# Retention in chunks, then eight experts: states multiplied in four quarters, the last logits in one go, and row writes moved earlier

## The chip, the cores and the metric

One core of a Trainium2 chip runs one program. The metric is device time in microseconds (us): the median over runs of the time of the whole program. One more execution was recorded by the profiler; every row and every time of a stage below is from that execution, counted from its first instruction.

## What is computed

The first half is a linear attention with decay (retention); the second is a layer of experts in which the pairs of token and expert are served in the order of their logits, each expert takes exactly 384 tokens, and each token goes to one expert.

```python
gamma = 1.0 - 2.0 ** (-5.0 - np.arange(H))            # B, H, S, D = 4, 8, 768, 64
for t in range(S):
    state = gamma * state + einsum('bhd,bhe->bhde', k[:, :, t], v[:, :, t])
    y[:, :, t] = scale * einsum('bhd,bhde->bhe', q[:, :, t], state)
x = y.transpose(0, 2, 1, 3).reshape(N, H * D)         # N = 3072 tokens of 512
logits = x @ w_gate                                   # E = 8 experts, cap = N // E = 384
for idx in np.argsort(-logits.flatten()):             # token idx // E, expert idx % E:
    ...                                               # taken if the token is free and counts[e] < cap
for e in range(E):
    out[assigned == e] = np.maximum(x[assigned == e] @ w1[e], 0) @ w2[e]
```

## The kernel before

**Units.** A sequence of 768 tokens is cut into six chunks of 128. A unit is one chunk of one of the four batches; unit u is chunk u // 4 of batch u % 4, so units 0 to 3 are the first chunk and 20 to 23 the last. `load(u)` brings a unit's keys, queries, values and keys again (1 MB; 768 KB in the last chunk) into one of eight buffers `ld`. Load u + 8 is issued when unit u is done, from SP, the one queue that also issues everything else of this stage.

**A unit's work.** `scores` multiplies keys with queries (TensorE, `sc`, two halves of the rows side by side), VectorE multiplies that with the decay (`am`), GpSimd scales queries and keys for the state (`qs`, `ks`). `outputs` multiplies the state `T[b]` with `qs` into the PSUM tile `yp`: per pair of heads a 128x128 matrix with the two heads' 64x64 states on its diagonal and zeros elsewhere. `mix` adds the values times `am` into the same tile, ScalarE copies it to `YS`, and keys times values go into `sp`, from which VectorE adds the next state into `T[b]`, in two instructions of 64 partitions per unit. The heads lie on partitions and the tokens on columns, so `YS` is the transposed x.

**Order.** TensorE, VectorE and ScalarE run in the written order of the loop over `groups`: eight groups of one unit, then eight of two. In each turn the scores of the next group are issued first, then `outputs`, then `aside()` (a small step of the routing), then `mix`. `gate(c)` makes the logits of a whole chunk with four matmuls side by side in 32 columns each; `gate_last` makes those of the last chunk unit by unit, 8 columns wide.

**Rows.** x has to lie in DRAM as rows, since the experts gather tokens from there. `row_blocks` turns 14 of the 24 units on VectorE into `xr` (a ring `xo` of six) and issues four writes of 64 KB each, called pieces below; `ROWS` says after which group. The other ten units are turned on TensorE (`row_out`) beside the first search for a threshold (`BESIDE`).

**Routing.** `span_parts` finds the range of the logits from the first `KNOWN` chunks; a search in three steps of 64 thresholds finds an expert's threshold, its tokens are numbered, x and the weights are gathered. After the last chunk comes the first count (`c0`), then the rest of the first search, which `BESIDE`, `HOT` and `WARM` fill with work or with multiplications of constants. From then on TensorE works through the eight experts, with the later searches beside it.

The SP queue gives each DMA one of eight semaphores in turn, so the ninth DMA in order waits until the first has landed.

Of the kernel before, what the change touches and what calls it, by code (L numbers as in the profile page):

```python
# [22 lines left out]
E = 8  # L23
# [23 lines left out]
LEFT = sum(k for k, _ in BESIDE)  # L47
# [6 lines left out]
def tile_retention_moe(ctx: ExitStack, tc: tile.TileContext, qkv, wg, idm, w1, w2,  # L54
# [15 lines left out]
    wgf = consts.tile([128, HP, 32], F32, name="wgf")  # L70
# [20 lines left out]

    def consts_on_chip():
        nc.vector.memset(onesb, 1.0)
# [5 lines left out]
        nc.vector.memset(un, 1.0)  # L99
        nc.vector.memset(zer512, 0.0)  # L100
        nc.vector.memset(Sc, 0.0)
        nc.vector.memset(Wq, 0.0)
        nc.vector.memset(bad, 0.0)
# [137 lines left out]
    xo = yctx.enter_context(tc.tile_pool(name="xo", bufs=6, side="right"))  # L241
# [9 lines left out]
    T = [rc.tile([128, HP, 128], F32, name=f"T{b}") for b in range(B)]  # L251
# [38 lines left out]
    def scores(u):  # L290
# [10 lines left out]
        qs = ks = None  # L301
        if c < NC - 1:
# [3 lines left out]
        if c:  # L306
            qs = rw.tile([128, HP, C], F32, name="qs", bufs=4)
            nc.gpsimd.tensor_tensor(qs.rearrange("p a b -> p (a b)"), q_,
                                    qtb[:, c].rearrange("p a b -> p (a b)"), op=OP.mult)
# [7 lines left out]

    def outputs(us):

        c = units[us[0]][1]  # L320
        for u in us:
            yp = yps[u] = rp.tile([128, HP, C], F32, name="yp", bufs=2)
            if c:
# [4 lines left out]
            else:  # L328
                busy(WARM[u + 1], yp[:, 0:2, :].rearrange("p a b -> p (a b)"))

    def mix(us):

        c = units[us[0]][1]
        for u in us:
            b, am, yp = units[u][0], st[u][0], yps.pop(u)
            v_ = LD[u][:, 2].rearrange("p (h d) -> p h d", h=H)
            for pr in range(HP):
                for s in range(2):
                    nc.tensor.matmul(yp[64 * s:64 * s + 64, pr, :], v_[:, 2 * pr + s, :], am[:, s, pr, :],  # L339
# [7 lines left out]
        if c < NC - 1:  # L347
# [13 lines left out]
    lt5 = []  # L361

    def gate_last(b):
        if not b:
            lt5.append(rp.tile([128, 64, E], F32, name="sp"))
        for pr in range(HP):
            nc.tensor.matmul(lt5[0][:, b, :], YS[b, NC - 1][:, pr, :], wgf[:, pr, 0:E], start=(pr == 0),
                             stop=(pr == HP - 1))
# [10 lines left out]
    def row_out(pr_, i):  # L379
        b, c = units[i]  # L380
        xr = xo.tile([128, DM], F32, name="xr")
        nc.scalar.activation(blocks(xr), pr_.rearrange("p (b a r) -> p b a r", a=4, b=HP), AF.Copy)
# [3 lines left out]
    def row_blocks(i):  # L386
# [6 lines left out]
        for a in range(4):  # L393
            nc.sync.dma_start(xs[t0:t0 + 128, 128 * a:128 * a + 128].rearrange("(t c) f -> c t f", t=4),
                              xr[32 * a:32 * a + 32].rearrange("p (t f) -> p t f", t=4))

    def gate(c):

        gl = rp.tile([128, 512], F32, name="gl")
        for pr in range(HP):  # L400
            for b in range(B):
                nc.tensor.matmul(gl[32 * b:32 * b + 32, 0:C], wgf[:, pr, :], YS[b, c][:, pr, :], start=(pr == 0),  # L402
# [23 lines left out]
    rowed = 0  # L426
    nu = len(units)
    groups = [[u] for u in range(2 * B)] + [[u, u + 1] for u in range(2 * B, nu, 2)]

    def aside():  # L430

        nonlocal parts, whole, ended
        if ended is not None:
            c, ended = ended, None
            logit(c)
            if c == 0:
                consts_on_chip()
# [726 lines left out]
```

## Time and profile before

| | |
|---|---|
| median of 3 runs | 443.43 us (442.95 to 445.39) |
| the profiled execution | 445.22 us, of which the span of its instructions 443.4 us |
| TensorE busy | 427.8 us (96%), granted clock 0.995 on average |
| VectorE, ScalarE, GpSimd busy | 300.8, 142.2, 142.9 us |
| retention, up to the first count's result | 0 to 104.8 us |
| first search, gathers | 104.8 to 124.2 us |
| eight experts | 124.2 us to the end |

The time around the span is 1.8 us in the profiled execution. TensorE is busy in nearly all of the span, so the chain of waits runs over it almost everywhere; but the stages have other limits beside it, which the rows below show. A row of the timeline gives the start, the length, engine, line, operation, the tiles written and read, the shapes, how many instructions are merged, and in brackets how long the engine had been idle and what ended that.

### The profile page before, as it was taken

Reading aid. Unit: us, or ns where it says so; the run is one execution under the profiler, and the core shown is the slowest. Engines: PE = TensorE matmul, PEld = TensorE weight load, DVE = VectorE, ACT = ScalarE, POOL = GpSimd, SP = SyncE. Lnnn points to the kernel's source line nnn. Section 1 sums busy time; section 2 is a strip of 40 time slices with the busy share of each in tenths; the row PEclk is TensorE's granted clock in tenths of the full one; section 3 lists DMA queues with packets and bytes.
Section 4 is the critical chain, followed back from the end, with each engine's and each line's share of the span. In section 5 each row is a group of like instructions: output and inputs, shape, how many; then the busy total and the mean of one; then the engine's idle time right before and its main releaser. Section 6 shows DMA issues by size and latency. Waiting matters only on the chain.

```text
span 443.4 us, 9124 instructions
## 1 busy us (share of the span) xinstructions
PE 427.8 (96%) x3745; PEld 372.2 (84%) x3747; DVE 300.8 (68%) x714; ACT 142.2 (32%) x221; POOL 142.9 (32%) x154
## 2 busy tenths in 40 slices
PE   9998999899989999999899999999999999999994
PEld 7887999898579778977797798789779989989983
DVE  1668689976798759875885888588668926416500
ACT  1111121203245226313431432434244436326301
POOL 2475665110340170034116216134103615402001
PEclk9999999998999999999999999999999999999999
DMA  7999888744673265138126436425703732831001
GB/s 256 410 414 417 328 261 259 215 92 132 237 231 127 97 191 236 27 133 312 54 95 218 186 120 212 169 59 167 296 26 119 229 152 77 302 143 47 1 25 53
DMA packets 23332, 78.99 MB, mean 178 GB/s; under 512 B 3058, under 2 KB 10866, under 8 KB 16884
## 3 DMA queue, kind: packets, MB, share of 16 engines
q0 software_dynamic: 8592, 46.14, 29.8%
q1 hardware_dynamic: 14692, 32.20, 20.7%
q8 instruction: 31, 0.51, 0.5%
q14 instruction: 17, 0.14, 0.1%
HBM read 65.75 MB, written 12.58 MB: 177 GB/s over the span
## 4 chain that ended last, share of the span: by engine, by line
PE 72%; issue 12%; DVE 9%; POOL 2%; DMA 1%; ACT 1%; POOLq 0%; SPq 0%; DVEq 0%
PE ph L869 22%; PE py L890 21%; PE psm L128 6%; PE sc L297 5%; PE yp L339 4%; PE yp L326 3%; PE ph L837 3%; PE sp L353 2%; DVE am L300 2%; POOL out L898 1%; PE gl L314 1%; DVE w2l L128 1%; POOL wraw L785 1%; DMA xg<-xs,idx 1%; PE gl L402 1%
## 5 line engine op out<-in xcount | busy, mean ns | idle before, releaser
L869 PE MATMUL ph<-xh,w1h 128*128 128x384 f32 x256 | 84.3, 343 | 0.5 <-ACT xh L842 0.5
L869 PE MATMUL ph<-xlo,w1h 128*128 128x384 f32 x256 | 82.7, 337 | 1.7 <-DVE xlo L128 1.5
L869 PE MATMUL ph<-xh,w1l 128*128 128x384 f32 x256 | 82.1, 335 | 0.0
L890 PE MATMUL py<-w2h,hh 128*128 128x512 f32 x192 | 78.9, 411 | 0.0
L890 PE MATMUL py<-w2l,hh 128*128 128x512 f32 x192 | 75.4, 393 | 0.6 <-DVE w2l L128 0.6
L890 PE MATMUL py<-w2h,hl 128*128 128x512 f32 x192 | 75.3, 392 | 0.0
L898 POOL DMA_INDIRECT out<-yo,oix x24 | 28.4, 1182 | 125.4 <-ACT yo L896 124.8
L873 ACT ACTIVATE hh<-ph 128x384 fp32r<-128x384 f32 x64 | 31.4, 491 | 77.5 <-PE ph L869 75.8
L785 POOL DMA_INDIRECT wraw<-w,wix x31 | 34.4, 1109 | 51.1 <-DVE un L128 38.1
L869 PEld LDWEIGHTS ph<-xlo,w1h 128*128 128x128 f32 x256 | 47.5, 188 | 2.3 <-DVE xlo L128 2.3
L869 PEld LDWEIGHTS ph<-xh,w1h 128*128 128x128 f32 x256 | 47.8, 188 | 1.6 <-ACT xh L842 0.7
L869 PEld LDWEIGHTS ph<-xh,w1l 128*128 128x128 f32 x256 | 47.7, 188 | 0.0
L128 DVE SCALAR_TENSOR_TENSOR hl<-ph,hh 128x384 fp32r<-128x384 f32 x64 | 34.7, 552 | 16.9 <-ACT hh L873 16.6
L128 DVE TENSOR_TENSOR w1l<-wraw,w1h 128x1024 fp32r<-128x1024 f32 (+1 forms) x36 | 39.2, 1099 | 7.1 <-ACT w1h L803 7.1
L890 PEld LDWEIGHTS py<-w2h,hl 128*128 128x128 f32 x192 | 36.0, 188 | 7.8
L890 PEld LDWEIGHTS py<-w2l,hh 128*128 128x128 f32 x192 | 36.2, 188 | 7.6 <-DVE w2l L128 1.7
L896 ACT ACTIVATE yo<-py 128x512 f32<-128x512 f32 x24 | 14.4, 598 | 86.6 <-PE py L890 47.1
L890 PEld LDWEIGHTS py<-w2h,hh 128*128 128x128 f32 x192 | 36.1, 188 | 6.9 <-issue 0.7
L824 POOL DMA_INDIRECT xg<-xs,idx x24 | 27.6, 1149 | 43.3 <-PE ph L869 28.7
L128 DVE TENSOR_TENSOR w2l<-wraw,w2h 128x1024 fp32r<-128x1024 f32 x32 | 38.7, 1217 | 1.7 <-ACT w2h L803 1.7
L803 ACT ACTIVATE w1h<-wraw 128x1024 fp32r<-128x1024 f32 (+1 forms) x36 | 33.7, 959 | 7.8 <-DMA wraw<-w,wix 7.8
L300 DVE TENSOR_TENSOR am<-sc,dm 128x512 f32<-128x512 f32 x48 | 30.1, 684 | 5.1 <-PE sc L297 4.7
(145 smaller groups left out, 613.2 us busy)
## 6 DMA issues: line engine op xcount, KB each, us to landing
ld<-qkv SPq DMA_DIRECT2D x19, 1024.0 KB, 9.5
xs<-xr SPq DMA_DIRECT2D x56, 64.0 KB, 3.9
ld<-qkv SPq DMA_DIRECT2D x4, 768.0 KB, 5.8
xs<-xr SPq DMA_DIRECT2D x10, 256.0 KB, 2.8
qtb<-qtab SPq DMA_DIRECT2D x5, 256.0 KB, 11.5
ld<-qkv SPq DMA_DIRECT2D x2, 512.0 KB, 5.2
wraw<-w,wix POOLq DMA_INDIRECT x33
xg<-xs,idx POOLq DMA_INDIRECT x24
```

Source lines behind the costliest of these rows:

```text
L128: return f(o, *a, **k)
L297: nc.tensor.matmul(sc[s][:, pr, :], k_[r, w], q_[r, w], start=True, stop=True)
L300: nc.vector.tensor_tensor(am[:, s], sc[s], dm[:, s], op=OP.mult)
L339: nc.tensor.matmul(yp[64 * s:64 * s + 64, pr, :], v_[:, 2 * pr + s, :], am[:, s, pr, :], start=(not c and pr == 0), stop=(pr == HP - 1), s ...
L785: nc.gpsimd.indirect_dma_start(out=t, out_offset=None, in_=w1v if nm == "w1" else w2v, in_offset=bass.IndirectOffsetOnAxis(ap=wix[:, hf:hf ...
L803: nc.scalar.activation(p[0], p[2], AF.Copy)
L824: nc.gpsimd.indirect_dma_start(out=t, out_offset=None, in_=xs, in_offset=bass.IndirectOffsetOnAxis(ap=found[n][0][:, j:j + 1], axis=0))
L869: nc.tensor.matmul(ph, a[:, o:o + 128], x_[:, d], start=(k == 0), stop=(k == 11))
L873: nc.scalar.activation(hh[:, f], ph, AF.Relu)
L890: nc.tensor.matmul(py, h_[:, f, t], a[:, o:o + DM], start=(k == 0), stop=(k == 23))
L896: nc.scalar.activation(yo, py, AF.Copy)
L898: sct = nc.gpsimd.indirect_dma_start(out=out, out_offset=bass.IndirectOffsetOnAxis(ap=oix[:, j:j + 1], axis=0), in_=yo, in_offset=None, bo ...
```

## The change

- `T[b]` holds the two heads' states one above the other in 64 columns. `outputs` multiplies each 64x64 state by itself: rows 0 to 63 or 64 to 127 of the array, and output partitions that are swapped for odd batches (`half`), so that the two units of a group address four different quarters. VectorE's addition is one instruction of 128 partitions. For odd batches the heads in `YS` are swapped; `wgf` has a second copy with swapped rows, and the row writes swap back.
- `gate_last` is gone; the last chunk has `gate(5)`, a copy by ScalarE and one transpose, with parts of the first count between them.
- Groups of two begin with the second chunk (14 groups instead of 16). `xo` has ten buffers. `ROWS` is {6: 4, 7: 1, 8: 3, 9: 2, 11: 2, 12: 2} instead of {8: 2, 9: 2, 10: 3, 11: 1, 12: 3, 14: 3}; the order of units is `TURNED`. One of the ten later units is turned right after the last logits, so `BESIDE` has nine.
- The range comes from two chunks. Zeros and ones are set at the very start, the casts of constants after the first chunk's last group. `qs` is issued before `ks`. `WARM` falls from (10, 4, 4, 4, 0) to (10, 2, 0, 0, 0), `HOT` rises from 22 to 25.

```diff
-WARM = (10, 4, 4, 4, 0)
+WARM = (10, 2, 0, 0, 0)
-KNOWN = 3
+KNOWN = 2
-ROWS = {8: 2, 9: 2, 10: 3, 11: 1, 12: 3, 14: 3}
-HOT = 22
-BESIDE = ((4, 0), (1, 0), (4, 0), (1, 0), (0, 6), (0, 10))
+ROWS = {6: 4, 7: 1, 8: 3, 9: 2, 11: 2, 12: 2}
+HOT = 25
+BESIDE = ((4, 0), (1, 0), (4, 0), (0, 1), (0, 6), (0, 10))
+TURNED = (1, 3, 5, 0, 7, 2, 4, 9, 11, 6, 13, 15, 17, 19)
...
-    T = [rc.tile([128, HP, 128], F32, name=f"T{b}") for b in range(B)]
+    T = [rc.tile([128, HP, D], F32, name=f"T{b}") for b in range(B)]
...
+    def half(s, b):
+        o = 64 * (s ^ (b & 1))
+        return slice(o, o + 64)
...
-                for pr in range(HP):
-                    nc.tensor.matmul(yp[:, pr, :], T[b][:, pr, :], qs[:, pr, :], start=(pr == 0), stop=False,
-                                     skip_group_check=True)
+        for pr in range(HP if c else 0):
+            for u in us:
                 b, qs = units[u][0], st[u][1]
+                for s in range(2):
+                    r = slice(64 * s, 64 * s + 64)
+                    nc.tensor.matmul(yps[u][half(s, b), pr, :], T[b][r, pr, :], qs[r, pr, :], start=(pr == 0),
+                                     stop=False, skip_group_check=True)
...
-                for s in range(2):
-                    r = slice(64 * s, 64 * s + 64)
-                    nc.vector.tensor_tensor(T[b][r, :, r], T[b][r, :, r], sp[r, i], op=OP.add)
+                nc.vector.tensor_tensor(T[b], T[b], sp[:, i], op=OP.add)
...
-    groups = [[u] for u in range(2 * B)] + [[u, u + 1] for u in range(2 * B, nu, 2)]
+    groups = [[u] for u in range(B)] + [[u, u + 1] for u in range(B, nu, 2)]
...
-        for u in groups[-1]:
-            gate_last(units[u][0])
         c = NC - 1
-        cols, Lc = slice(c, COLS, NC), lt5[0][:, 0:B]
+        gate(c)
...
+        first(0, 8)
+        lt = rp.tile([128, 512], F32, name="sp")
+        nc.tensor.transpose(lt[:, 0:128], gs[c % 2], ident)
+        cols, Lc = slice(c, COLS, NC), lt[:, 0:128].rearrange("p (b x) -> p b x", b=B)[:, :, 0:E]
+        first(8, COLS - B)
         f = best(Lc, cols, m0, oh0)
+        pr_ = rp.tile([128, DM], F32, name="sc1", bufs=2)
+        row_part(pr_, rest[0], 0, HP)
+        row_out(pr_, rest.pop(0))
         reach(cols, B, m0, cmp0, grid[0])
         f()
...
+        first(COLS - B, COLS)
```

The SP queue before, from the load of units 12 to 15 on (`ld` 128x2048 or 128x1536 are loads of one unit, `xs<-xr` 32x4x128 are pieces of rows):

```order
L268 DMA ld<-qkv 128x2048 x4
L276 DMA qtb<-qtab 128x512
L268 DMA ld<-qkv 128x2048 x2
L394 DMA xs<-xr 32x4x128 x8
L268 DMA ld<-qkv 128x2048 x2
L276 DMA qtb<-qtab 128x512
L394 DMA xs<-xr 32x4x128 x8
L268 DMA ld<-qkv 128x1536 x2
L394 DMA xs<-xr 32x4x128 x12
L268 DMA ld<-qkv 128x1536 x2
L394 DMA xs<-xr 32x4x128 x28
```

The same place in the changed kernel:

```order
L270 DMA ld<-qkv 128x2048 x4
L278 DMA qtb<-qtab 128x512
L270 DMA ld<-qkv 128x2048 x2
L398 DMA xs<-xr 32x4x128 x16
L270 DMA ld<-qkv 128x2048 x2
L278 DMA qtb<-qtab 128x512
L398 DMA xs<-xr 32x4x128 x4
L270 DMA ld<-qkv 128x1536 x2
L398 DMA xs<-xr 32x4x128 x12
L270 DMA ld<-qkv 128x1536 x2
L398 DMA xs<-xr 32x4x128 x24
```

Between the loads of units 16 and 17 and those of 18 and 19 now stand sixteen pieces instead of eight; ahead of the last load there are 32 instead of 28.

TensorE before, at the end of the retention: the states of units 22 and 23, the logits of the two units before, a transpose, `mix`, and the logits of the last two units.

```order
L326 MATMUL yp<-qs,T_109 128x128 x4
L326 MATMUL yp<-qs,T_110 128x128 x4
L367 MATMUL sp<-wgf,ys_5_1354 128x8 x4
L367 MATMUL sp<-wgf,ys_5_1365 128x8 x4
L408 MATMUL gl<-ident,gs_142 128x128
L339 MATMUL yp<-am,ld 64x128 x16
L367 MATMUL sp<-wgf,ys_5_1440 128x8 x4
L367 MATMUL sp<-wgf,ys_5_1451 128x8 x4
```

The same place in the changed kernel, up to the first four of sixteen matmuls of `gate(5)`:

```order
L337 MATMUL yp<-qs,T_109 64x128 x2
L337 MATMUL yp<-qs,T_110 64x128 x2
L337 MATMUL yp<-qs,T_109 64x128 x2
L337 MATMUL yp<-qs,T_110 64x128 x2
L412 MATMUL gl<-ident,gs_142 128x128
L348 MATMUL yp<-am,ld 64x128 x16
L406 MATMUL gl<-ys_5_1400,wgf 32x128
L406 MATMUL gl<-ys_5_1411,wgf 32x128
L406 MATMUL gl<-ys_5_1479,wgf 32x128
L406 MATMUL gl<-ys_5_1490,wgf 32x128
```

The states' products alternate between the two units, two heads at a time; the logits of the last chunk all come after `mix`, in the form that the other chunks had already.

## Rows read from the trace of the kernel before

**Rows 1.** The page: busy us by engine; one kind of DMA, us from issue to landing

```profile
PE 427.8 (96%) x3745; PEld 372.2 (84%) x3747; DVE 300.8 (68%) x714; ACT 142.2 (32%) x221; POOL 142.9 (32%) x154
...
xs<-xr SPq DMA_DIRECT2D x10, 256.0 KB, 2.8
```

**Rows 2.** Timeline of TensorE, one turn of the loop (units 12 and 13)

```profile
57.51 2.06 PE L297 MATMUL sc<-ld 64*128 64x128 f32 x32
59.50 2.05 PE L326 MATMUL yp<-qs,T 128*128 128x128 f32 x16
61.48 1.97 PE L339 MATMUL yp<-am,ld 128*64 128x128 f32 x32
63.28 1.10 PE L353 MATMUL sp<-ld,ks 128*64 128x64 f32 x32
64.31 1.08 PE L402 MATMUL gl<-ys,wgf 128*32 128x128 f32 x32
```

**Rows 3.** Timeline of TensorE, from the last scores to the first count's result

```profile
88.70 2.06 PE L297 MATMUL sc<-ld 64*128 64x128 f32 x32
...
97.46 1.85 PE L367 MATMUL sp<-wgf,ys 128*128 128x8 f32 x16
...
99.41 1.97 PE L339 MATMUL yp<-am,ld 128*64 128x128 f32 x32
101.30 1.95 PE L367 MATMUL sp<-wgf,ys 128*128 128x8 f32 x16
...
104.79 0.16 PE L128 MATMUL psm<-sg,onesb 64*128 64x1 bf16 x1 [0.43 <-DVE sg L128]
```

**Rows 4.** Timeline of the SP queue's issues (the third row from a shorter window)

```profile
49.28 0.80 SPq L268 DMA_DIRECT2D ld<-qkv  x2
52.20 6.83 SPq L394 DMA_DIRECT2D xs<-xr  x8
58.73 0.30 SPq L394 DMA_DIRECT2D xs<-xr  x1
59.15 0.87 SPq L268 DMA_DIRECT2D ld<-qkv  x2
60.59 9.25 SPq L394 DMA_DIRECT2D xs<-xr  x8
69.95 0.93 SPq L268 DMA_DIRECT2D ld<-qkv  x2
79.92 0.88 SPq L268 DMA_DIRECT2D ld<-qkv  x2
```

**Rows 5.** Waits of the SP queue, 0 to 125 us: total us, times, longest

```profile
SPq L394 <- DMA ld<-qkv: 12.3, 6, 3.3
```

**Rows 6.** Timeline of GpSimd: units 7, 9 and 23, each started as its load landed

```profile
28.54 1.04 POOL L304 TENSOR_TENSOR ks<-ld,ktb 128x512 f32<-128x512 f32 x1 [0.38 <-DMA ld<-qkv]
...
34.19 1.04 POOL L304 TENSOR_TENSOR ks<-ld,ktb 128x512 f32<-128x512 f32 x1 [0.19 <-DMA ld<-qkv]
...
88.64 1.35 POOL L308 TENSOR_TENSOR qs<-ld,qtb 128x512 f32<-128x512 f32 x1 [1.96 <-DMA ld<-qkv]
```

**Rows 7.** Windows: us, busy by engine, granted clock, DMA engines' busy share, GB/s

```profile
40.00:45.00 5.00, 5.00 (x79) 4.57 (x76) 3.92 (x8) 0.60 (x1) 2.72 (x3) 1.00 1.02 415
...
105.00:110.00 5.00, 5.00 (x46) 4.58 (x47) 3.00 (x9) 2.46 (x5) 0.00 (x0) 0.68 0.44 161
```

**Rows 8.** Groups by form, 40 to 104 us: busy us, mean ns, idle before

```profile
L359 DVE TENSOR_TENSOR T<-T,sp 64x256 f32<-64x256 f32 x26 | 10.9, 418 | 7.1 <-PE sp L353 6.9
...
L343 ACT ACTIVATE ys<-yp 128x256 f32<-128x256 f32 x4 | 1.5, 384 | 10.8 <-PE yp L339 10.8
...
L404 ACT ACTIVATE gs<-gl 128x128 f32<-128x128 f32 x4 | 1.1, 278 | 4.9 <-PE gl L402 4.9
```

**Rows 9.** Timeline of TensorE: rows turned in the first search, early and late

```profile
105.79 1.06 PE L373 MATMUL py<-ident,ys 128*128 128x128 f32 x4
...
110.42 0.60 PE L373 MATMUL ph<-ident,ys 128*128 128x128 f32 x4
```

More of the change, by code (lines that the diff above doesn't have):

```diff
@@ L381, in row_out @@
         xr = xo.tile([128, DM], F32, name="xr")
-        nc.scalar.activation(blocks(xr), pr_.rearrange("p (b a r) -> p b a r", a=4, b=HP), AF.Copy)
+        to, of = blocks(xr), pr_.rearrange("p (b a r) -> p b a r", a=4, b=HP)
+        if b & 1:
+            for z in range(2):
+                nc.scalar.activation(to[:, :, 2 * z:2 * z + 2], of[:, :, 2 - 2 * z:4 - 2 * z], AF.Copy)
+        else:
+            nc.scalar.activation(to, of, AF.Copy)
         t0 = (b * NC + c) * 128
@@ L426, in tile_retention_moe, with aside @@
     rowed = 0
+    rest = [u for u in range(len(units)) if u not in TURNED]
+    rest.sort(key=lambda u: (u & 1, u))
     nu = len(units)
-    groups = [[u] for u in range(2 * B)] + [[u, u + 1] for u in range(2 * B, nu, 2)]
-    def aside():
+    groups = [[u] for u in range(B)] + [[u, u + 1] for u in range(B, nu, 2)]
+    def aside(g):
         nonlocal parts, whole, ended
[L433 to L437, printed above, removed]
-            cols = slice(c, COLS, NC)
+        new = ended
+        if new is not None:
+            logit(new)
+            cols = slice(new, COLS, NC)
             best(L[:, cols], cols, m0, oh0)()
@@ L441, in aside @@
             whole.append(cols)
-            if c == KNOWN - 1:
+            ended = None
+            if new == KNOWN - 1:
                 parts = list(span_parts(rc, rp))
-        if parts:
+                parts.pop(0)()
+        elif parts:
             parts.pop(0)()
-        elif parts == []:
+            return
+        if parts == [] and (new is None or g == len(groups) - 1):
             for cols in whole:
@@ L464, in tile_retention_moe @@
             outputs(us)
-            if g > B:
-                if g == len(groups) - 1:
-                    for u in groups[g - 1]:
-                        gate_last(units[u][0])
-                aside()
-            mix(us)
-            if g in (B - 1, B):
+            if g == B:
                 for u in ahead:
                     st[u] = scores(u)
+            if g > B:
+                aside(g)
+            mix(us)
+            if g == B - 1:
+                for u in ahead:
+                    st[u] = scores(u)
+                consts_on_chip()
             for u in us:
@@ L484, in tile_retention_moe, with first @@
                     ended = c1
[L485 to L486 removed]
         c = NC - 1
[L488 removed]
+        gate(c)
+        c0 = rp.tile([1 << QB[0], E], F32, name="sc0", bufs=2)
+        order = [c for k in range(NC) for c in range(k, COLS, NC)]
+        def first(k0, k1):
+            for k in range(k0, k1):
+                nc.tensor.matmul(c0, cmp0[:, order[k], :], oh0[:, order[k], :], start=(k == 0), stop=(k == COLS - 1))
+        first(0, 8)
[3 more added lines that the diff above has]
+        first(8, COLS - B)
         f = best(Lc, cols, m0, oh0)
+        pr_ = rp.tile([128, DM], F32, name="sc1", bufs=2)
+        row_part(pr_, rest[0], 0, HP)
+        row_out(pr_, rest.pop(0))
         reach(cols, B, m0, cmp0, grid[0])
         f()
[L492 removed]
         sg0 = sw.tile([1 << QB[0], E], BF, name="sg")
[L494 to L496 removed]
+        first(COLS - B, COLS)
         nc.vector.tensor_copy(L[:, cols], Lc)
```

71 lines of the change are left out of this document (30 added, 41 removed).

## The prediction

> **What bounds the kernel now.** I read the page first, for the engine that the chain runs over, then the timeline of TensorE, then the queue that brings the loads. TensorE is busy for 96% of the span [rows 1], so in the experts, whose instructions stand in the same order in both kernels, nothing is to be won: what changes is the time at which they start. One turn of the retention loop shows how that stage is made up: scores 2.0 us, states 2.0, `mix` 1.8, new states 1.0, each from start to start, and a gate of 1.0 in every second turn [rows 2]. The last `mix` begins at 99.41, and the first count's result goes out at 104.79 [rows 3].
>
> The second view is the SP queue. The reader is to see that it is not free: eight pieces of rows took 6.83 and 9.25 us between two pairs of loads, because the eighth piece could only go out at 58.73, when an earlier load had landed [rows 4]; pieces waited 12.3 us for loads in all [rows 5]. Loads 18 and 19 were issued at 59.15, 20 and 21 at 69.95, 22 and 23 at 79.92 [rows 4], and unit 23's data came at 88.64 [rows 6], just when its scores were due [rows 3]. The DMA engines were full at 415 GB/s around 40 to 45 us [rows 7], which makes 2.5 us of a load of 1 MB and 1.9 of one of 768 KB.
>
> **The change, part by part.**
>
> *States in quarters.* Before, eight instructions of 128x128 per unit take 1.0 us, 2.0 for a pair. Now a pair has 32 instructions of a quarter's size. The nearest row is the gate: 32 instructions of the same 128 columns, in four parts of the array beside each other, in 1.08 us [rows 2]; I take 1.0 for a pair. The other bound is the scores' row, where 32 instructions run two beside each other: 2.0, so no gain. No row shows two halves of the rows writing into one PSUM tile, as the quarters of one unit do; the scores' halves go to two tiles.
>
> The Trainium skill (TensorEngine Tiling, Restrictions and Gotchas) says that different row tiles cannot use the same PSUM bank at the same time. By that rule the quarters of one unit would take turns and a pair would stay at 2.0; it is the second rival below, and no run so far shows it.
>
> VectorE's addition of 256 columns costs 0.42 on 64 partitions [rows 8]; I take the same on 128, so 20 fewer of them are 8 us of VectorE in the stage. It is no longer near the bound, so I book this, the constants and the smaller range at zero on the path; they lie in VectorE's waits for loads.
>
> *TensorE if nothing else held it.* Fewer multiplications of constants cost and gain nothing: the first units wait for loads either way. Load 7 lands at 28.54 [rows 6]; scores of unit 7 end at 29.5, `mix` and new states of units 4 and 5 at 32.3. Unit 8's scores follow, unit 9's wait for 34.19 [rows 6] and end at 35.2. States 1.0, a transpose 0.2, `mix` and new states 2.8 give 39.2; one turn of 5.8 gives 45.0. There units 8 and 9 are done and loads 16 and 17 can go out, 4.3 us before the old 49.28. With a gate and three turns of 6.0, and another gate, TensorE wants units 18 and 19 at 65.0.
>
> *The queue of loads.* Here the change adds a wait: sixteen pieces instead of eight now stand ahead of loads 18 and 19.
> - From 34.2 on the DMA engines still have six loads (15 us) and two tables of 256 KB (1.3) to bring: 50.5. Loads 16 and 17 make that 55.5.
> - A piece delays a load beside it. From 49.28 to 58.73 passed 9.45 us [rows 4]: 5.0 for the two loads, 2.2 between issue and landing that is no transfer (2.8 for 256 KB, less 0.6 [rows 1]), and 2.3 for seven pieces, 0.33 each. Bounds: nothing, and 1.16 (9.25 by eight). Six pieces go out before load 17 has landed: 57.5.
> - The eighth piece waits for that landing; then nine pieces at 0.42 (58.73 to 59.15 [rows 4]): loads 18 and 19 are issued at 61.3, against 59.15 before.
> - Load 19 lands after 2.2 + 5.0 + four pieces, 1.3: 69.8. Unit 19's scores could have begun at 66.0: a wait of almost 4 us, with `mix`, GpSimd's scaling and every later turn behind it. Scores end at 70.8, the turn and its gate at 75.9.
> - Loads 20 and 21 land behind it: a table 0.6, 3.8 for both, six or seven pieces 2.2, 76.4, hardly late. TensorE is through the next turn at 82.0 and wants units 22 and 23.
> - Five of the twelve pieces wait for load 21 and need 2.3: loads 22 and 23 go out at 79, where they did before. From 79.92 to 88.64 they took 8.7; so unit 23 is there at 87.8, its scores end at 88.8. TensorE waits almost 5 us.
>
> *From the last load on.* States 1.0, `mix` 1.9, gate 1.0, states 1.0, transpose 0.2, `mix` 1.9: 95.8. Before, that `mix` ended at 101.3. Gain **5.5**, of which 2.0 come from the two states, 1.7 from `gate_last` (97.46, 1.85 long with its overlap [rows 3]) leaving this place, the rest from the last scores, which before ended at 90.7 (88.70 and 2.0 [rows 3]).
>
> *The last logits.* Before, from 101.3 to 104.79: 3.5. Now: copy of the last unit 0.4 [rows 8] and a hop 0.1, gate 1.0, ScalarE's copy 0.3 [rows 8], transpose 0.3, twelve counts 0.55 (24 took 1.1, from 103.25 to 104.36 [rows 3]), a unit of rows 0.6 [rows 9], four counts 0.2, VectorE and hops 0.6: 4.05. Loss **0.6**; between 0.2 and 1.2 (rows at 1.06, all of the last copy waited for).
>
> *The clock.* The first four units of rows in the search took 1.06 instead of 0.60 [rows 9], at a granted clock of 0.68 on average over 105 to 110 [rows 7], which is about 3.2 us at the lower of the two levels. Ahead of it TensorE had 3.5 us of matmuls only 8 columns wide. That stretch is now broken by a gate and a unit of rows; I take it that the clock stays: the second count comes **1.0** earlier (bounds 0 and 1.05). One unit of rows less in the search, 0.6 against a filler of 0.2: **0.3**, since it stood before a small matmul that VectorE waits for. The larger `HOT` lies in the wait for the gather; ten buffers in `xo` remove no wait that VectorE's timeline shows; swapped heads cost a second instruction on ScalarE, which is idle. Nothing for these; the larger `wgf` brings 64 KB more, under 0.2 us of an early load.
>
> **The sum.** 5.5 - 0.6 + 1.0 + 0.3 = 6.2 less what the waits make of the rough edges, 0.3: 5.9 us. Span 443.4 to 437.5; the profiled execution (445.22) would show 439.3. The median lies 1.8 below that execution; the same 5.9 off it gives **437.5**.
>
> **The rivals.**
> - *The loads hardly hold.* If pieces cost nothing beside loads, load 17 lands at 55.5, load 19 at 66.6, 21 and 23 in time, and TensorE's last `mix` ends at 88: 429.4 at best; half of it done, 432.5. For it: a piece alone is small. Against: three rounds in [rows 4] took 10 us each.
> - *Quarters two at a time.* 1.0 more per pair; under the waits for loads most is hidden, but two pairs come after load 23: 2.0 more, 439.5.
> - *The clock falls in the waits for loads.* In each TensorE has one unit's scores in almost 5 us. At the lower level for 3.2 us it loses 1.6; after unit 19 that vanishes in the next wait, after unit 23 it is on the path: 439.1. The Trainium skill (TensorE: Matmul & The Clock Gate, HAM oscillation) says that waits for DMA between short pieces of TensorE work bring the clock down. The row of 105 to 110 agrees that thin work does; a wait for a load that did it is in no row.
> - *The queue gets slower.* If a piece behind a landed load takes 1.16 us instead of 0.42, nine of them move loads 18 and 19 to 68, load 21 to 83, five more move the last pair to 89 and unit 23 to 97.5: `mix` ends at 105.5, and the time is 447. It decides from 0.85 us per piece on. For it: 9.25 us for eight. Against: that holds the waits for two loads.
>
> **Chances.** Forecast 0.45 (436 to 440), loads hardly hold 0.18, two at a time 0.15, clock 0.15, slower queue 0.07. A measurement of this kernel can tell about 0.5%, 2.2 us. Faster by more: 0.45 + 0.18, and 0.11 each of the next two (their upper ends come near no change), 0.85; within: 0.09; slower: 0.06, the slower queue. The range 431.5 to 441.0 leaves out the best end of the second case, the worst of the two smaller gains, and the slower queue.
>
> **What would show it.** Right: a pair's states at about 1.0; SP issuing loads 18 and 19 after 60 us; TensorE idle for about 4 us before the scores of unit 19 and of unit 23; unit 23's scores near 88; the first count's result at 99 to 100; the rows in the search at 0.60; the experts as long as before. Wrong: no such idle time (loads), states at 2.0 (quarters), a granted clock near 0.5 at 70 or 88 us, or 20 pieces by 67 us taking over 0.85 each.

## The result, and the profile after

The changed kernel took 438.54 us as the median of four runs (436.61 to 442.83), against 444.41 us (442.95 to 445.64) for the kernel before: a ratio of 0.9889, 95% interval 0.984 to 0.9938. Taken a second time it gave 0.9893 (0.9857 to 0.9929). Its profiled execution took 439.00 us, with a span of 437.2 us. The forecast was 437.5 us. The ratios leave out runs that are more than 1.5% above the fastest of the same kernel; of the kernel "quarters, ten buffers" below these are seven of twelve, and the median of all its runs, 442.14 us, is that of the kernel before on that chip, 442.11.

**The page**, busy us by engine, to be set beside [rows 1]:

```profile
PE 416.9 (95%) x3902; PEld 359.2 (82%) x3902; DVE 289.2 (66%) x694; ACT 142.5 (33%) x224; POOL 141.3 (32%) x154
```

TensorE is busy for 11 us less, but the span fell by only 6.2. The difference is new idle time, 3.1 us of it from 65 to 100 us and 1.3 ahead of 40 us.

**Timeline of TensorE**, one turn of the loop (the units 12 and 13 of [rows 2]), then the turns of units 18 to 21, then the end of the retention as in [rows 3]:

```profile
55.71 1.10 PE L337 MATMUL yp<-qs,T 64*64 64x128 f32 x32
56.75 0.27 PE L214 MATMUL gl<-ident,ext 128*2 128x128 f32 x1
56.95 1.97 PE L348 MATMUL yp<-am,ld 128*64 128x128 f32 x32
58.74 1.10 PE L362 MATMUL sp<-ld,ks 128*64 128x64 f32 x32
59.78 1.08 PE L406 MATMUL gl<-ys,wgf 128*32 128x128 f32 x32
...
68.11 1.16 PE L299 MATMUL sc<-ld 64*128 64x128 f32 x16 [1.15 <-DMA ld<-qkv]
71.51 1.58 PE L299 MATMUL sc<-ld 64*128 64x128 f32 x16 [2.24 <-DMA ld<-qkv]
73.02 1.98 PE L337 MATMUL yp<-qs,T 64*64 64x128 f32 x32
...
79.29 2.06 PE L299 MATMUL sc<-ld 64*128 64x128 f32 x32
...
86.91 1.16 PE L299 MATMUL sc<-ld 64*128 64x128 f32 x16 [0.34 <-DVE xr L393]
...
93.32 1.97 PE L348 MATMUL yp<-am,ld 128*64 128x128 f32 x32
...
99.33 0.17 PE L130 MATMUL psm<-sg,onesb 64*128 64x1 bf16 x1 [0.44 <-DVE sg L130]
99.44 0.65 PE L371 MATMUL ph<-ident,ys 128*128 128x128 f32 x4
```

A pair's states take 1.04 us from start to start (55.71 to 56.75), where [rows 2] had 1.98. At 68 and 71 us the idle time in brackets is new: TensorE waits 1.15 and 2.24 us for the loads of units 18 and 19. The states behind them take 1.98, twice their time. The last `mix` begins at 93.32 instead of 99.41 and the first count's result goes out at 99.33 instead of 104.79. The rows turned in the search take 0.65 or 0.60, where [rows 9] had 1.06 first.

**Windows of TensorE** (us, busy, granted clock, DMA engines' busy share, GB/s), around the doubled states, and in the search as the second row of [rows 7]:

```profile
72.00:73.00 1.00, 1.00 (x13) 0.54 1.00 418
73.00:75.00 2.00, 2.00 (x35) 0.50 0.99 409
...
105.00:110.00 5.00, 4.93 (x45) 1.00 0.65 240
```

From 72 to 75 us the clock is at the lower level, behind the two waits; in the search it stays at the upper one.

**The SP queue**: its issues, as in [rows 4]:

```profile
45.39 1.01 SPq L270 DMA_DIRECT2D ld<-qkv  x2
47.23 15.38 SPq L398 DMA_DIRECT2D xs<-xr  x16
62.72 0.89 SPq L270 DMA_DIRECT2D ld<-qkv  x2
...
64.17 2.38 SPq L398 DMA_DIRECT2D xs<-xr  x4
66.66 1.76 SPq L270 DMA_DIRECT2D ld<-qkv  x2
71.45 8.20 SPq L398 DMA_DIRECT2D xs<-xr  x12
79.76 0.87 SPq L270 DMA_DIRECT2D ld<-qkv  x2
```

Its waits for loads, as in [rows 5] (us in total, times, longest):

```profile
SPq L398 <- DMA ld<-qkv: 13.7, 7, 3.7
```

GpSimd's start on unit 23, as in [rows 6]:

```profile
86.93 1.30 POOL L306 TENSOR_TENSOR qs<-ld,qtb 128x512 f32<-128x512 f32 x1 [0.65 <-DMA ld<-qkv]
```

The sixteen pieces fill the queue from 47 to 62.6 us, and loads 18 and 19 go out behind them. The last loads leave at 79.76, where they left at 79.92 before. Unit 23's data comes 1.7 us earlier (86.93 against 88.64): from the issue of the last pair it took 7.2 us, where it took 8.7 before. In the timeline of TensorE the profile puts the wait of 0.34 us at 86.91 down to VectorE's turning of a row, which the scores do not use; since GpSimd started on unit 23 at that moment as its load landed, it is read here as a wait for that load.

**Groups by form**, VectorE's addition to the state, to be set beside [rows 8]:

```profile
L366 DVE TENSOR_TENSOR T<-T,sp 128x256 f32<-128x256 f32 x14 | 5.2, 416 | 7.6 <-PE sp L362 7.6
```

So 256 columns cost the same on 128 partitions as on 64.

Where the 6.2 us of the span come from, by stage: the last `mix` ends at 95.29 instead of 101.38 (6.1 won); from there to the first count's result 4.04 instead of 3.41 (0.6 lost); from there to the first product of the gathered tokens, at 117.46 instead of 124.22, 18.13 instead of 19.43 (1.3 won); the experts last 319.74 instead of 319.18 (0.6 lost).

### The profile page after: what moved, and what is told of

The parts are those of the page before. It is cut to its first block, busy times and chain, and to the rows that moved or that the text cites. A ratio compares the mean times of both kernels' runs of the same rounds, so it can differ in the third digit from the quotient of the medians.

```text
span 437.2 us, 9426 instructions
## 1 busy us (share of the span) xinstructions
PE 416.9 (95%) x3902; PEld 359.2 (82%) x3902; DVE 289.2 (66%) x694; ACT 142.5 (33%) x224; POOL 141.3 (32%) x154
## 4 chain that ended last, share of the span: by engine, by line
PE 58%; DMA 14%; issue 13%; DVE 6%; SPq 3%; POOL 3%; ACT 1%; POOLq 0%; DVEq 0%; ACTq 0%
PE ph L887 23%; PE py L908 21%; DMA ld<-qkv 12%; PE psm L130 6%; PE ph L855 2%; SPq L398 2%; PE yp L348 2%; DMA xs<-xr 1%; POOL out L916 1%; DVE w2l L130 1%; DMA xg<-xs,idx 1%; POOL wraw L803 1%; PE sc L299 1%; PE yp L337 1%; DVE cmp L130 1%
## 5 line engine op out<-in xcount | busy, mean ns | idle before, releaser
L803 POOL DMA_INDIRECT wraw<-w,wix x31 | 33.0, 1066 | 48.5 <-DVE un L130 35.6
```

Of the source, the lines that this page charges most:

```text
L803: nc.gpsimd.indirect_dma_start(out=t, out_offset=None, in_=w1v if nm == "w1" else w2v, in_offset=bass.IndirectOffsetOnAxis(ap=wix[:, hf:hf ...
```

## The experiments

The theory: the end of the retention is set by loads that stand on the SP queue behind pieces of rows, so that the quarters' saving is mostly swallowed by waits for loads, apart from what comes behind the last load. First rival: the loads hardly bind, and the quarters count in every turn. Second rival: the fall of the clock in the waits is what costs.

All runs are in one table. The first two columns come from each kernel's profiled execution: the start of the first count's result and that of the first product of gathered tokens. The ratio is that of the times to the kernel before on the same chip.

| kernel | first count | gathered | ratio, 95% interval |
|---|---|---|---|
| before | 104.79 | 124.22 | 1 |
| changed | 99.33 | 117.46 | 0.9889, 0.984 to 0.9938 |
| changed, again | 100.13 | 119.11 | 0.9893, 0.9857 to 0.9929 |
| logits alone | 102.53 | 120.49 | 0.9943, 0.9914 to 0.9973 |
| quarters alone | 102.01 | 121.47 | 0.9939, 0.9906 to 0.9972 |
| quarters, ten buffers | 103.92 | 123.36 | 0.991, 0.9869 to 0.995 |
| changed, whole states | 102.05 | 120.11 | 0.9943, 0.9912 to 0.9974 |
| changed, waits filled | 99.11 | 117.07 | 0.9879, 0.9836 to 0.9922 |
| changed, rows of eight units first | 109.92 | 127.67 | 1.0107, 1.0063 to 1.0152 |
| changed, rows late | 100.48 | 117.89 | 0.9938, 0.9909 to 0.9968 |
| changed, loads first | 96.54 | 117.32 | 0.9829, 0.9784 to 0.9875 |
| changed, second queue | 98.24 | 116.04 | 0.9876, 0.9836 to 0.9916 |
| changed, one unit a turn there | 94.72 | 112.60 | 0.9773, 0.9728 to 0.9817 |
| changed, pieces one turn later | 94.84 | 112.76 | 0.9777, 0.9728 to 0.9825 |

One profile per kernel can be off by itself: the two of the changed kernel differ by 0.80 us at the first count and by 1.65 at the gathered tokens, so that differences of a microsecond or two between rows of this table are not sure. In the profile of "loads first" the clock was at 0.50 from 120 to 125 us and the experts lasted 323.2 us; its rows are read up to the gather, and its ratio.

### The parts by themselves

**Logits alone.** The kernel before with `gate(5)` and the counts in parts instead of `gate_last`:

```diff
...
-        for u in groups[-1]:
-            gate_last(units[u][0])
...
+        gate(c)
...
+        first(0, 8)
...
+        nc.tensor.transpose(lt[:, 0:128], gs[c % 2], ident)
...
+        first(8, COLS - B)
...
```

> The kernel before the change with the new treatment of the last logits alone: gate of the whole last chunk, one transpose, the first count in parts between them, but no unit of rows turned there. States whole, groups, rows, constants, range as before. Theory: 1.7 us of the small matmuls leave TensorE ahead of the last mix, 0.1 to 0.6 is lost behind it, and the rows in the search take 0.6 instead of 1.06 us if the clock stays full (1.0 to 1.3 won): about 2.5 us below the kernel before, with the last mix ending at 99.6. Rival (this part gives nothing, everything came from the states): the same time as before within 1 us.

Its last `mix`, in the timeline of TensorE:

```profile
96.70 1.97 PE L339 MATMUL yp<-am,ld 128*64 128x128 f32 x32
```

It ended at 98.67, the first count's result came 2.26 us earlier and the gathered tokens 3.73: 1.47 of it lies in the search, where all rows took 0.60 to 0.66 at full clock. By the stages this is somewhat more than expected; by the ratio of 0.9943 it is some 2.5 us, as expected.

**Quarters alone**, and the same with ten row buffers:

```diff
...
-                    nc.tensor.matmul(yp[:, pr, :], T[b][:, pr, :], qs[:, pr, :], start=(pr == 0), stop=False,
-                                     skip_group_check=True)
...
+                for s in range(2):
+                    r = slice(64 * s, 64 * s + 64)
+                    nc.tensor.matmul(yps[u][half(s, b), pr, :], T[b][r, pr, :], qs[r, pr, :], start=(pr == 0),
+                                     stop=False, skip_group_check=True)
...
-    xo = yctx.enter_context(tc.tile_pool(name="xo", bufs=6, side="right"))
+    xo = yctx.enter_context(tc.tile_pool(name="xo", bufs=10, side="right"))
```

> The kernel before with the states in quarters alone (with swapped heads, the second copy of the gate's weights and the state's addition in one instruction); logits, groups, rows, buffers, constants and range as before. Theory: the earlier turns gain nothing, since the scores of units 18, 19 and 22, 23 wait for their loads, which come when they did (unit 23's at 88.6); left are the two pairs behind the last load and a little of the loads that leave earlier: 2 to 3 us below the kernel before. Rival (each of the eight pairs and four single units counts): 8 us and more below.

The size was right, 2.8 us at both stages, and the place was not, so that the size was in part luck: TensorE waited for no load. Timelines of VectorE and then of TensorE with six buffers:

```profile
77.87 0.71 DVE L400 STREAM_TRANSPOSE xr<-ys 128x512 f32<-128x512 f32 x1 [1.91 <-DMA xs<-xr]
```

```profile
81.11 0.38 PE L218 MATMUL gl<-ident,topb 2*128 2x2 f32 x2 [2.45 <-DVE L L420]
81.42 3.63 PE L346 MATMUL yp<-am,ld 128*64 128x128 f32 x32
```

VectorE waited 1.91 us for a row buffer, since the pieces of an earlier row had not landed; the logits' copy behind it was late, TensorE waited 2.45 for that, and `mix` then ran at half speed. The last `mix` did so too, behind the 8-column matmuls of `gate_last` that this kernel still has (3.58 us at 95.00, where the kernel before took 1.97).

> The run with the quarters alone, with ten buffers in xo instead of six. There VectorE waited 1.91 us for a row buffer whose pieces had not landed, TensorE 2.45 us for VectorE behind it, and the granted clock fell. Theory (of the two things that were late there, buffer and last load, the load is late next): VectorE's wait for a row buffer and most of TensorE's 2.45 us go, units 22 and 23 then wait for their loads, which land at 84.4 and 86.4 as before, so the scores of unit 23 move by less than 0.6 us; in all the first count's result comes 0 to 0.6 us earlier, and another 1.7 only if the clock then stays full in the last mix. Rival (the six buffers alone held the quarters' gain): 2 to 2.5 us earlier at the scores of units 22 and 23, with no wait for a load.

Timeline of TensorE with ten buffers:

```profile
79.23 0.38 PE L218 MATMUL gl<-ident,topb 2*128 2x2 f32 x2 [0.65 <-DVE L L420]
...
85.66 1.17 PE L297 MATMUL sc<-ld 64*128 64x128 f32 x16 [3.22 <-DMA ld<-qkv]
87.58 2.08 PE L297 MATMUL sc<-ld 64*128 64x128 f32 x16 [0.76 <-DMA ld<-qkv]
```

VectorE's wait for a buffer is gone, and TensorE's behind it fell to 0.65. In their place stand 3.22 and 0.76 us for the loads of units 22 and 23, which came a good microsecond later than with six buffers. Nothing was won at these scores: behind the buffer stood the load. The first count's result came 1.9 us later than with six buffers, not 0 to 0.6 earlier, since the last pair's loads came later and the clock fell behind the waits for them (the scores took 2.08 at 87.58). The interval of the ratio can't tell the two kernels apart.

**Whole states** in the changed kernel (eight row buffers, for space):

```diff
-                for s in range(2):
-                    r = slice(64 * s, 64 * s + 64)
-                    nc.tensor.matmul(yps[u][half(s, b), pr, :], T[b][r, pr, :], qs[r, pr, :], start=(pr == 0),
-                                     stop=False, skip_group_check=True)
+                nc.tensor.matmul(yps[u][:, pr, :], T[b][:, pr, :], qs[:, pr, :], start=(pr == 0), stop=False,
+                                 skip_group_check=True)
```

> The changed kernel with the states as before the change: 128x128 matrices of two heads with zeros beside them, eight instructions of 128 rows per unit, the state's addition in two instructions, no swapped heads (xo has eight buffers instead of ten, for space). A pair's states take 2.0 us instead of 1.03. Theory (most of what the quarters save goes into waits for loads): only the two pairs behind the last load cost, the waits of 2.2 and 1.2 us before units 18 and 19 shrink, and the time is 2 to 4 us above the changed kernel's, about 441.5. Rival (the quarters' saving counts in every turn, eight pairs at 1.0 and more): 8 us and more above, 446 or later.

It lost 2.7 us at both stages against the first profile of the changed kernel, and by the ratios 2.2 to 2.4, with intervals that overlap a little: the direction and the size that the theory said. Of the 2.7, 1.66 lie behind the start of unit 23's scores, where the theory had all of it; the other 1.06 lie ahead of it, as that unit's data came 1.1 us later. Its waits of TensorE for loads in the retention:

```profile
PE sc L299 <- DMA ld<-qkv: 1.4, 2, 0.8
```

There are 1.4 us of such waits where the changed kernel has 3.4. There are ten pairs, so about 10 us of matmul time were put back, and 2.7 of them came out at the end.

Logits alone and quarters alone add up to 6.48 us at the gathered tokens, of the 6.76 that the whole change won there. That only 0.3 is left for constants, buffers, range, groups and rows together is not shown: the second profile of the changed kernel won 5.11 there, and "quarters alone" holds losses that the whole change does not have (the wait for a buffer, and the last `mix` at the lower clock).

### What the loads do

**Rows of eight units first:** 32 pieces instead of 16 ahead of loads 18 and 19.

```diff
-ROWS = {6: 4, 7: 1, 8: 3, 9: 2, 11: 2, 12: 2}
+ROWS = {6: 8, 8: 2, 11: 2, 12: 2}
```

> The changed kernel with the rows of eight units instead of four turned after units 8 and 9, so that 32 pieces instead of 16 stand ahead of loads 18 and 19 (none is added in all). Theory: sixteen more pieces at 0.4 us each put the issue of loads 18 and 19 from 62.7 to about 69, unit 19 lands at about 77 instead of 71.5; since 8 fewer pieces stand ahead of the last pair, half of that is won back, and the time is 3 to 6 us above the changed kernel's, 442 to 445. Rival (loads do not bind): the same time within 1 us.

Its SP queue with the queue's waits for VectorE's rows (us, times, longest), its TensorE, and a window of all engines, with the granted clock third from the end:

```profile
48.08 24.49 SPq L398 DMA_DIRECT2D xs<-xr  x32
72.68 0.87 SPq L270 DMA_DIRECT2D ld<-qkv  x2
...
SPq L398 <- DVE xr L393: 2.3, 3, 1.1
```

```profile
78.05 2.08 PE L299 MATMUL sc<-ld 64*128 64x128 f32 x16 [9.52 <-DMA ld<-qkv]
```

```profile
75.00:80.00 5.00, 1.95 (x16) 1.81 (x16) 0.00 (x0) 0.00 (x0) 1.93 (x2) 0.50 0.98 403
```

The direction was right and the size too small: the loads went out at 72.68, not 69, since the row of pieces took 9.1 us longer than the sixteen of the changed kernel (24.49 against 15.38), 0.57 for each further piece, where 0.4 was taken. At least 1.6 of the 9.1 us are longer waits for VectorE to turn the rows, 2.3 us where the changed kernel's row of pieces had 0.7; that leaves 0.47 a piece. The clock at 0.50 from 75 to 85 us added to it. The kernel is slower than the one before: what the rival of the slower queue foretold came about here, by more pieces and not by slower ones.

**Rows late**, at the places of the kernel before:

```diff
-ROWS = {6: 4, 7: 1, 8: 3, 9: 2, 11: 2, 12: 2}
+ROWS = {6: 2, 7: 2, 8: 3, 9: 1, 10: 3, 12: 3}
```

> The changed kernel with rows turned after the same units as before the change (two, two, three, one, three, three units instead of four, one, three, two, two, two, the first three sets one turn later than the changed kernel's): eight pieces instead of sixteen stand ahead of loads 18 and 19, 28 instead of 32 ahead of the last. Theory (moving the rows earlier took part of the quarters' gain away): loads 18 and 19 are issued at about 59 instead of 62.7, the wait for unit 19 shrinks from 2.2 us to under 0.5 and the clock stays full there; the last load is issued 1 to 2 us earlier: first count at 97.5 to 98.5 instead of 99.3, the time about 1.3 us less. Rival (moving the rows earlier is what won time, by clearing the queue for the last load and the gather): 1 us and more above.

Half of the theory's expectation held: loads 18 and 19 left at 56.60 and nothing waited for them. The rest failed, as its SP queue and its TensorE show:

```profile
78.65 1.83 SPq L270 DMA_DIRECT2D ld<-qkv  x2
```

```profile
85.20 1.63 PE L299 MATMUL sc<-ld 64*128 64x128 f32 x16 [4.09 <-DMA ld<-qkv]
87.14 2.08 PE L299 MATMUL sc<-ld 64*128 64x128 f32 x16 [0.31 <-DMA ld<-qkv]
```

The last two loads left only 1.1 us earlier and took the queue 1.83 us instead of 0.87, and the whole wait now stood at the last units, 4.09 and 0.31 us, with the lower clock behind it, on the path. The first count came 1.15 us later than in the changed kernel's first profile, 0.35 later than in its second, and the interval of the ratio overlaps both of that kernel's: the expected gain is absent, a loss is not shown. Leaving earlier did not bring the last data earlier either: GpSimd started on unit 23 at 87.16, 8.5 us after the issue, where the changed kernel took 7.2; what sets that time is open. Over these kernels the last pair left later the more pieces stood ahead of it: with 20 (one turn later) at 71.80, with 28 at 78.65 (rows late) and 79.92 (the kernel before), with 32 (the changed kernel) at 79.76, with 40 (eight units first) at 85.64. No run changes that number alone.

**Waits filled** with multiplications of constants:

```diff
+        busy({18: 8, 19: 18}.get(u, 0), sc[0][:, 0:2, :].rearrange("p a b -> p (a b)"))
```

> The changed kernel with multiplications of constants on TensorE (8 and 18 of 256 columns, about 0.9 and 1.9 us) ahead of the scores of units 18 and 19, where it waits 1.15 and 2.24 us for loads and the granted clock then falls to 0.50. Theory: the clock stays full, the states of units 18 and 19 take 1.0 instead of 1.98 us and TensorE is 1.4 us earlier at units 20 and 21, but the data of unit 23 comes at 86.8 all the same, where its scores already began at 86.9: the time moves by less than 0.6 us. Rival (the fall of the clock is on the path): 1.4 us less from unit 18 to the end.

The states behind the scores of units 18 and 19 took 1.10 (they are those of units 16 and 17, since a turn begins with the next pair's scores), the clock stayed at 1.00, the scores of units 20 and 21 began 1.06 us earlier, at 78.23. And then, in the timeline of TensorE:

```profile
73.05 1.10 PE L338 MATMUL yp<-qs,T 64*64 64x128 f32 x32
...
84.75 1.16 PE L300 MATMUL sc<-ld 64*128 64x128 f32 x16 [0.34 <-DMA ld<-qkv]
86.69 1.16 PE L300 MATMUL sc<-ld 64*128 64x128 f32 x16 [0.78 <-DMA ld<-qkv]
```

TensorE gave back 0.34 and 0.78 us in new waits for the last loads; 0.2 us was left at the first count. The rival of the clock falls for this place.

**Loads first:** pieces are held (`held_rows`) and issued by `write_rows`, which is called from the turn of units 14 and 15 on, behind the loads of units 22 and 23.

```diff
...
-            nc.sync.dma_start(xs[t0:t0 + 128, f0:f0 + 128].rearrange("(t c) f -> c t f", t=4),
-                              xr[32 * a:32 * a + 32].rearrange("p (t f) -> p t f", t=4))
+        held_rows.append((b, t0, xr))
...
+            if g >= 9:
+                write_rows()
```

> The changed kernel, with VectorE turning the same rows at the same places, but their pieces are put on the SP queue only behind the loads of units 22 and 23 (40 pieces in one burst, then the rest as before). Theory (the loads held behind pieces set the end of the retention): no wait of TensorE for a load from unit 16 on, the granted clock stays full there, the last mix ends at 88 to 90 us instead of 95.2, and the time is 5 to 7 us below the changed kernel's, about 432. Rival (the loads do not bind, the quarters' saving is all there already): last mix at 95, the same time within 1 us.

Its last `mix` and its first gathered tokens, in the timeline of TensorE:

```profile
90.53 1.97 PE L348 MATMUL yp<-am,ld 128*64 128x128 f32 x32
...
117.32 0.66 PE L864 MATMUL ph<-ident,xg 128*128 128x128 f32 x4 [3.19 <-DMA xg<-xs,idx]
```

The edit did not put all pieces behind the last loads: in the SP queue as it ran nine of the forty stood ahead of them, two ahead of loads 20 and 21 and seven between those and the last pair. No wait for a load was left and the clock stayed full up to the gather, but the last `mix` ended at 92.5, not 88 to 90: a turn took 6.1 us without a gate and 7.2 with one, and twice TensorE stood idle for 0.7 to 0.9 us for which the profile names no releaser. And the gain was lost at the gather, which waited 3.19 us for its tokens: the row writes left the queue until 107.6. By the ratio it is 0.6% better than the changed kernel, within the intervals.

### A kernel without the wait

**A second queue:** the pieces of eight units issued from ScalarE, two units a turn; then those of four units, one a turn.

```diff
...
+            if 6 < g < 11:
+                write_rows(nc.scalar, 2)
```

> The changed kernel with the row pieces taken out of the loads' way: those of the first eight units turned are issued from ScalarE's queue, two units a turn, one turn after VectorE turned them; those of the other six stay on the SP queue, behind the loads of units 22 and 23. So nothing stands ahead of a load, and the pieces are not late as they were with all of them behind the loads. Theory (two limits, the loads behind pieces and then the rate at which SP issues pieces): no wait for a load from unit 16 on, last mix at about 90 as with the loads first, the first count's result at 96 to 97, and no added wait at the gather, which begins at about 114.5 instead of 117.5: about 3 us below the changed kernel. Rival (ScalarE's issuing holds up its copies, on which TensorE waits): waits for gs and ys appear in each turn, and the time is the changed kernel's or above.

Waits of ScalarE with two units a turn (us, times, longest), and the row of TensorE behind one of them:

```profile
ACT ys L355 <- DMA xs<-xr: 20.1, 3, 8.6
```

```profile
86.43 1.58 PE L337 MATMUL yp<-qs,T 64*64 64x128 f32 x32 [1.50 <-ACT ys L355]
```

No load was late, but both sides were seen: ScalarE's copies stood behind its own pieces, and TensorE once behind a copy. It gained 1.4 us at the gathered tokens; the ratio shows no gain.

> As the run with the second queue, but ScalarE's queue issues only the four units turned after units 8 and 9, one a turn (four pieces); the rest goes on the SP queue behind the loads of units 22 and 23. Theory (in the run before ScalarE's copies stood up to 6 us behind eight pieces that waited for a semaphore that an earlier DMA held): with four pieces a turn the wait of TensorE for a copy (1.50 us there) goes, no load is late, the first count's result comes at 96.5 to 97.5 and the gather at 114.5 to 115.5, 2 to 3 us below the changed kernel in the stages. Rival (any piece on ScalarE's queue holds its copies up): waits for ys or gs remain and the gather begins at 116 or later.

With four pieces a turn the wait for a copy went, and the stages came earlier than expected, at 94.72 and 112.60. The rest of the pieces is on SP; nine of them stood ahead of the last pair of loads, which left at 70.49. Its ratio, 0.9773, is that of the next kernel.

**Pieces one turn later**, on SP alone:

```diff
...
+            write_rows()
             for _ in range(ROWS.get(g, 0)):
                 row_blocks(TURNED[rowed])
                 rowed += 1
+            if g >= 9:
+                write_rows()
```

> The changed kernel with each piece on the SP queue one turn later than VectorE turned its rows: behind the loads that the next turn issues (after units 14 and 15 at once again). Sixteen pieces stand between loads 18, 19 and 20, 21 instead of ahead of 18, 19, and twenty in all ahead of the last load instead of 32. Theory (a load is late only by the pieces ahead of it, and there is slack behind loads 18 and 19): loads 18 and 19 go out at about 53 and land by 61, no wait for a load from unit 16 on, last mix ends at 92.5 as with all loads first, first count's result at 96.5; the last pieces go out 5 us earlier than there, so the gather begins at 114.5 to 115 instead of 117.5: 2.5 to 3 us below the changed kernel, about 436. Rival (the SP queue is too full for any order: the gather is late again): gather at 117 or later.

Its SP queue, and its TensorE:

```profile
45.70 7.92 SPq L270 DMA_DIRECT2D ld<-qkv  x4
...
54.19 14.09 SPq L405 DMA_DIRECT2D xs<-xr  x16
68.39 0.86 SPq L270 DMA_DIRECT2D ld<-qkv  x2
69.34 2.34 SPq L405 DMA_DIRECT2D xs<-xr  x4
71.80 1.33 SPq L270 DMA_DIRECT2D ld<-qkv  x2
```

```profile
88.83 1.97 PE L348 MATMUL yp<-am,ld 128*64 128x128 f32 x32
...
94.84 0.17 PE L130 MATMUL psm<-sg,onesb 64*128 64x1 bf16 x1 [0.43 <-DVE sg L130]
...
112.76 0.65 PE L865 MATMUL ph<-ident,xg 128*128 128x128 f32 x4 [0.35 <-DMA xg<-xs,idx]
```

The same sixteen pieces now stand behind loads 18 and 19, which leave with 16 and 17 in one row of four, and the twelve that stood ahead of the last pair now stand behind it; what each of the two moves brought was not run by itself. The last loads go out 8 us earlier, at 71.80, TensorE waits for no load, and the gather is not late. It won 4.5 us at the first count and 4.7 at the gathered tokens over the changed kernel, more than the 2.5 to 3 expected. At 432.54 us, where the kernel before took 442.08 on that chip, it beats both kernels: 0.9777, its interval's upper end (0.9825) below the lower end of the changed kernel's second measurement (0.9857).

**The changed kernel again:**

> The changed kernel once more, unaltered, as the measure for the other runs: the same stage times as in its first profile within 0.5 us, about 438.5 us.

The ratio was the same, 0.9893. The stages were not within 0.5 us: the first count came at 100.13 and the gathered tokens at 119.11, with the clock at 0.66 from 100 to 105 us. At the last loads its TensorE waited for nothing:

```profile
86.25 2.06 PE L299 MATMUL sc<-ld 64*128 64x128 f32 x32
```

GpSimd started on unit 23 at 86.82, ahead of that unit's scores in this row. Here TensorE was the later of the two, by about 0.4 us.

## Why the prediction was right, step by step

- **States in quarters: right.** A pair takes 1.04 us. The rival of two at a time falls. The Trainium skill's rule behind it (TensorEngine Tiling, Restrictions and Gotchas), that different row tiles cannot use one PSUM bank at the same time, did not set the time here: the two halves of the rows of one unit write into one tile `yp`, and 32 such products of two units take 1.04 us, as the 32 of the gate do. The measurement decides.
- **The queue of loads: right in kind, off in its terms.** "Nine pieces at 0.42" took 5.35 us instead of 3.8 (from the eighth at 57.37 to loads 18 and 19 at 62.72), so that unit 19's scores waited until 71.5 and not 69.8. One of the nine took 1.47 us, the median one 0.45. The wait itself was 1.15 + 2.24 us, where 4 were forecast, since TensorE came to unit 18 at 66.96 and not at 65.0. The sign that was named for the slower queue, 20 pieces by 67 us at over 0.85 each, was met by the letter (15.38 + 2.38 us, 0.89 each), but it was badly chosen: 7.1 us of that time are the queue's waits for loads to land, and loads 18 and 19 went out at 62.72, not at 68.
- **"TensorE waits almost 5 us" before unit 23: wrong.** It waited 0.34. By the test named in the prediction this spoke for the first rival. The reason was another: TensorE itself came to units 20 and 21 at 79.29 instead of 75.9, by the late load 19 (1.7 us) and by the clock (about 1.5), so that it met the last loads just as they landed, at 86.9 (forecast 87.8). The filled waits show that they bound there: 1.06 us won ahead of them left 0.2. They bound only just, for in the second profile TensorE came 0.4 us behind the load. That the forecast of the landing came out within a microsecond is in part luck: the last pair left 0.8 us later than forecast and took 7.2 us instead of 8.7. The rows of the kernel before were read a little wrong too: its unit 23 had its data at 88.64, but the scores that began at 88.70 are those of unit 22, and TensorE waited for no load there.
- **The clock: it fell where it was said to cost nothing**, behind the wait for unit 19, and there it cost little: with the clock full and the waits filled 0.2 us was won. On the path, at the last units, it fell in the kernel with late rows, where the wait was 4.09 us.
- **From the last load on, and the last logits: right.** The last `mix` ended at 95.3 (95.8), the loss behind it was 0.63 (0.6).
- **The clock in the search, one row less: right by size, 1.3 us, but not certain.** The rows took 0.60 to 0.66 in the first profile and in all nine experiments with the new logits, and over 1 us at first in all three kernels with the old ones; but in the changed kernel's second profile the clock fell there with the new ones too.
- **Edits booked at zero:** no run shows them by themselves, and the 0.3 us that the parts' sum leaves is below the difference between two profiles. Ten buffers are no edit without effect, though: with the quarters and six buffers VectorE does wait for one.
- **The experts:** 0.6 us longer, where no change was forecast; the stage is the same in all these kernels and lasted 317.4 to 323.2 in their other profiles. In the total it is offset by the last `mix`, which ended 0.5 us earlier than forecast, and by the 0.3 booked for rough edges.
- **The rival "loads hardly hold"** gave 429.4 at best for TensorE without waits for loads, with the last `mix` ending at 88. With the pieces one turn later the kernel comes near that case: its last `mix` ended at 90.8, and its time was 432.54. That it needs another order of the queue shows that loads did hold in the changed kernel.

## What to carry to other kernels

When one engine becomes faster in a loop, look at what each queue still has ahead of the next load: here ten pairs at 1 us each gave some 2.5 us, until writes that could wait a turn stood behind the loads, which brought 4.5 us more. A write's place in a queue has two deadlines, the loads behind it and its own reader: with most of them behind the last loads the gather was late, one turn later met both. And a wait that is taken away only pays as far as the next thing that is late, be it a buffer or a load.

## What the runs showed of the hardware

- Issuing a piece of 64 KB cost the SP queue 0.44 us in the median (the 32 of "eight units first"), near the 0.42 between two neighbours; single ones took up to 2.25 us (in "one turn later"; 1.47 at 60.17 in the changed kernel), so that the nine ahead of loads 18 and 19 took 0.59 each. What makes those long is open.
- From the issue of the last pair of loads to GpSimd's start on unit 23 passed 7.2 us (the changed kernel) to 8.7 (the kernel before). What sets this is open.
- The granted clock fell to 0.50 behind two waits of 1.15 and 2.24 us with one unit's scores between them, and stayed at 1.00 in the kernel with whole states, whose wait there was 0.85.
- The same program's time scattered by some 6 us (436.61 to 442.83 for the changed kernel) with the mean granted clock (0.997 and 0.990 in these two). We estimate that the clock makes about half of it: 0.7% of 441 us is 3.1 us. Where the rest comes from is open.
- DMAs issued from ScalarE held its own copies up for 20.1 us in three waits at eight pieces a turn; at four a turn its copies had no such wait.
